# Weighted experts: the first product's 7-for-8 scheme beside the second's, in 64x64 pieces of the array, with packed weights

## The chip, the cores and the metric

The kernel runs on one core of one Trainium2 chip. A time is device microseconds of one execution. TensorE is written PE, its weight loads PEld, VectorE DVE, ScalarE ACT, GpSimd POOL, and SyncE, which issues most DMAs, SP. All data are fp32.

## The reference, cut to what matters

```
q_p, k_p = phi(q), phi(k)                   # 64 features: outer product of two 8-wide projections
x = (q_p @ (k_p.T @ v)) / (q_p @ sum(k_p))  # 4 batches, 4 heads, 1088 tokens, 32 wide
x: (4352, 128)                              # the heads side by side
P = exp(x @ w_gate - max)                   # 8 experts
8 times: P /= row sums; P /= column sums; P *= 4352 / 8
out = sum over e of P[:, e] * (relu(x @ w1[e]) @ w2[e])   # w1 128 x 1024, w2 1024 x 128
```

Every token goes through every expert, so the two products of the experts are nearly all of the arithmetic. Because P is positive, P[:, e] may be multiplied into x ahead of the first product.

## The kernel before

**Layout.** xT holds x transposed: 128 features on the partitions, 4352 tokens along the free axis. The first product of one expert takes 128 columns of w1 as weights and streams tokens: the hidden values come out with 128 of the 1024 hidden units on the partitions. The second product takes 128 rows of w2 as weights and streams hidden values. Every matmul is issued as two halves of 64 output columns, at positions (0, 0) and (0, 64) of the array (128 rows by 64 columns each), and the trace shows each fp32 half as two MATMUL and two LDWEIGHTS instructions.

**Three stretches.** First attention, batch by batch (`attention(b)`), with POOL and SP turning its result into xT (`take_over`, L486 and L488). Then `routing()`: the logits and 8 rounds of row and column sums, small work on DVE. Where attention and routing leave PE free, the generator `steps()` fills in expert work that needs no P (calls of `fill(n)`): expert 0 for all tokens, and expert 1 for the first 1280. This is the plain phase; its results, unweighted, wait in `kept`. At the end of routing P goes to DRAM as `pT`, and the weighted phase does the rest: experts 1 to 7 for the tokens from 1280 on, experts 2 to 7 below. In it x is multiplied by its weights, broadcast from `pT` by a DMA, on POOL (`prepare_x`, L678).

**The weighted phase before.** Groups of 3 tiles of 256 tokens. `four(k)` computes the first product in the ordinary way (`first`, L914), four blocks of 128 hidden units at a time; ACT applies the relu out of PSUM (L918). The second product of 4 hidden blocks by 2 output halves by 3 token tiles would be 24 half-size products; `twenty(k)` does it with 20, from sums of hidden values (DVE, L978 and L998) and sums of blocks of w2 (`sums_of_four`: POOL once for each expert, L242, then stored in DRAM and loaded back for each group). `into` (L1099) accumulates them in PSUM, `part_of_twenty` combines the sums at a group's end. The last group has 2 tiles of 256 and 7 products for 8 in the second product (`seven`), with sums of w2 from `sums_of_two` (POOL, L203 to L206).

**Queues.** DVE, PE and ACT run an order written by hand (`tc.manual_schedule`). POOL and SP are in-order queues. An instruction in `tc.keep_in_program_order(...)` is pinned behind the instruction traced before it on its engine. The buffers of the early phases (`phs`, two tiles, and `rb`) are read by attention until its last matmuls L462, at 96.8 us. The code that runs as routing ends is:

```
        for n in routing():
            fill(n)
        early.close()
        pools.append(ctx.enter_context(tc.tile_pool(name="late", bufs=2)))
        prepare_x(PLAIN)
        fill(8)
    for _ in work:
        pass
```

Of the kernel before, what the change touches and what calls it, by code (L numbers as in the profile page):

```python
# [18 lines left out]
def f64_to_f32(nc, pool, raw, shape):  # L19


    p, n = shape
    low, high = raw[:, 0::2], raw[:, 1::2]

    def u32(name):
        return pool.tile([p, n], U32, name=name)

    def f32(name):
        return pool.tile([p, n], F32, name=name)
# [21 lines left out]
def kernel(  # L51
# [31 lines left out]
    wpool = ctx.enter_context(tc.tile_pool(name="wpool", bufs=2))  # L83
# [5 lines left out]
    hb = big.tile([P, 9600], F32, name="hb")  # L89
    early = ExitStack()  # L90
    ld = early.enter_context(tc.tile_pool(name="ld", bufs=2))
    wk = early.enter_context(tc.tile_pool(name="wk", bufs=2))

# [93 lines left out]
    def load_w(e, sums=True, again=False):  # L187
        w1 = wpool.tile([P, F], F32, tag="w1", name="w1")
        w2 = wpool.tile([P, FO, DM], F32, tag="w2", name="w2")
        nc.sync.dma_start(out=w1, in_=moe_w1[e])  # L190
        nc.sync.dma_start(out=w2, in_=moe_w2[e].rearrange("(fo fi) d -> fi fo d", fi=P))
        return w1, w2, sums_of_two(e, w2, again) if sums else None

    def sums_of_two(e, w2, again=False):

        ws = wpool.tile([P, 4, FO // 2, H2], F32, tag="ws", name="ws")
        if e in stored:
            nc.sync.dma_start(out=ws, in_=stored[e])
            return ws
        a11, a21 = w2[:, 0::2, 0:H2], w2[:, 0::2, H2:DM]  # L200
        a12, a22 = w2[:, 1::2, 0:H2], w2[:, 1::2, H2:DM]
        keep_ = tc.keep_in_program_order if e < 2 else lambda x: x
        keep_(nc.gpsimd.tensor_tensor(ws[:, 0], a21, a22, op=Alu.add))  # L203
        keep_(nc.gpsimd.tensor_tensor(ws[:, 1], ws[:, 0], a11, op=Alu.subtract))
        keep_(nc.gpsimd.tensor_tensor(ws[:, 2], a11, a21, op=Alu.subtract))
        keep_(nc.gpsimd.tensor_tensor(ws[:, 3], a12, ws[:, 1], op=Alu.subtract))  # L206
        if again:
            stored[e] = dram.tile([P, 4, FO // 2, H2], F32, name=f"ws{e}")
            nc.sync.dma_start(out=stored[e], in_=ws)
        return ws  # L210

    stored, stored_four = {}, {}

    FOURS = (((5, 6), ((0, 0), (0, 2)), ((1, 0), (1, 2)), True),
             ((4, 10), ((1, 0), (1, 2)), ((1, 1), (1, 3)), False),
             ((12, 7), ((0, 0), (0, 2)), ((0, 1), (0, 3)), False),
             ((11, 14), ((0, 2), (1, 2)), ((0, 1), (0, 1)), True),
             ((1, 16), ((0, 0), (1, 0)), ((0, 3), (0, 3)), True),  # L220
             ((15, 13), ((0, 1), (0, 3)), ((1, 0), (1, 2)), False),
             ((2,), ((1, 3),), ((0, 3),), True), ((3,), ((1, 1),), ((0, 1),), True),
             ((8,), ((1, 1),), ((1, 2),), True), ((9,), ((1, 3),), ((1, 0),), True))
    FORMS = [n for ns, *_ in FOURS for n in ns]

    def sums_of_four(e, w2):

        ws = pools[0].tile([P, len(FORMS), FO // 4, H2], F32, tag="ws4", name="ws4")
        if e in stored_four:
            nc.sync.dma_start(out=ws, in_=stored_four[e])  # L230
            return ws

        def blocks(bs):
            b = w2[:, bs[0][1]::4, H2 * bs[0][0]:H2 * (bs[0][0] + 1)].unsqueeze(1)
            if len(bs) == 1:
                return b
            step = (bs[1][1] - bs[0][1]) * DM + (bs[1][0] - bs[0][0]) * H2
            return AP(tensor=b.tensor, offset=b.offset, ap=[b.ap[0], [step, 2], *b.ap[2:]])

        c = 0  # L240
        for ns, x, y, off in FOURS:
            tc.keep_in_program_order(nc.gpsimd.tensor_tensor(ws[:, c:c + len(ns)], blocks(x), blocks(y),  # L242
                                                             op=Alu.subtract if off else Alu.add))
            c += len(ns)
        stored_four[e] = dram.tile([P, len(FORMS), FO // 4, H2], F32, name=f"ws4{e}")
        nc.sync.dma_start(out=stored_four[e], in_=ws)
        return ws


# [5 lines left out]
    def projections():  # L255
        flat = raw.rearrange("p n d -> p (n d)")
        s12 = f64_to_f32(nc, consts, flat, (P, 2 * D)) if words == 2 else flat.bitcast(F32)
# [25 lines left out]
    both = consts.tile([P, H2], F32, name="both")  # L283
    nc.gpsimd.tensor_tensor(both, ident[:, 0:H2], ident[:, H2:DM], op=Alu.add)
# [3 lines left out]
    first_w = load_w(0, False)  # L288
# [282 lines left out]
    def routing():  # L571
# [22 lines left out]
        for it in range(ITERS):  # L594
# [7 lines left out]
            nc.vector.reduce_sum(cs, p1.rearrange("p g e -> p e g"), axis=AX.X)  # L602
            yield 4.25
# [13 lines left out]
        for b in (1, 0, 2, 3):  # L617
# [9 lines left out]
    NMAX = 512  # L627
# [4 lines left out]
    groups = [(0, 256, 2, [0], False), (512, 288, 2, [0], False), (0, 256, 2, [1], False),  # L632
              *((1088 + 832 * i, 416, 2, [0], False) for i in range(3)), (3584, 384, 2, [0], False),
              (512, 384, 2, [1], False)]
    PLAIN = len(groups)
# [3 lines left out]
    for lo in (1280, 512, 2048, 2816, 3584):  # L639
        groups.append((lo, NT3, 3, list(range(2 if lo == 512 else 1, E)), True))  # L640
    groups.append((0, 256, 2, list(range(2, E)), True))
    assert sorted((lo, e) for lo, n, t, es, _ in groups for lo in range(lo, lo + n * t, 32) for e in es) == [
        (lo, e) for lo in range(0, N, 32) for e in range(E)]
    kept = [keep.tile([P, N], F32, name="kept0"), keep.tile([P, 1280], F32, name="kept1")]
    items = [(g, e) for g, group in enumerate(groups) for e in group[3]]
    loaded_w, sources, sums, parts, done = {}, {}, {}, {}, {}
# [5 lines left out]
    def tiles_of(j):  # L652
        return groups[items[j][0]][2]

    def prepare_w(j):
        g, e = items[j]
        three = groups[g][2] == 3
        if j == 0:
            loaded_w[j] = first_w
        elif items[j - 1][1] == e or not groups[g][4]:  # L660
            before = [i for i in range(j) if items[i][1] == e and i in loaded_w]
            loaded_w[j] = loaded_w[before[-1]] if before else load_w(e, False)
            if three and tiles_of(j - 1) == 2:
                loaded_w[j] = *loaded_w[j][0:2], sums_of_four(e, loaded_w[j][1])
        else:
            loaded_w[j] = load_w(e, not three, again=groups[g][4])
            if three:
                if g == len(groups) - 2 and e in groups[-1][3]:
                    sums_of_two(e, loaded_w[j][1], True)
                loaded_w[j] = *loaded_w[j][0:2], sums_of_four(e, loaded_w[j][1])  # L670

    def weights_of(e, lo, n, tag):
        pb = pools[0].tile([P, 3 * NT3], F32, tag=tag, name=tag)[:, 0:n]
        tc.keep_in_program_order(nc.sync.dma_start(out=pb, in_=pT[e:e + 1, lo:lo + n].to_broadcast([P, n])))
        return pb

    def weigh(out, x, pb):
        tc.keep_in_program_order(nc.gpsimd.tensor_tensor(out, x, pb, op=Alu.mult))  # L678

    def prepare_x(j):  # L680
        g, e = items[j]
        lo, n, t, es, weighted = groups[g]
        x = xT[:, lo:lo + t * n]
        if not weighted:
            sources[j] = x
            return
        xe = weights_of(e, lo, t * n, "xe")
        for sl in (slice(0, 512), slice(512, 768)) if j == first_weighted else (slice(0, t * n),):
            weigh(xe[:, sl], x[:, sl], xe[:, sl])
        sources[j] = xe  # L690

    first_weighted = next(j for j, (g, e) in enumerate(items) if g == PLAIN)

    def weigh_kept(g, i):

        lo, n, t, es, _ = groups[g]
        ys = [kept[e][:, lo:lo + n * t] for e in range(es[0])]
        if i < len(ys):
            weigh(ys[i], ys[i], weights_of(i, lo, n * t, "pb"))
            return  # L700
        for y in ys[1:]:
            tc.keep_in_program_order(nc.gpsimd.tensor_tensor(ys[0], ys[0], y, op=Alu.add))
        if t == 2:
            k1, k2 = ys[0][upper, 0:n], ys[0][upper, n:2 * n]
            tc.keep_in_program_order(nc.gpsimd.tensor_tensor(k1, k1, k2, op=Alu.subtract))
# [5 lines left out]
    def put(y, lo, n, queues):  # L711
        b0, nb = lo // 32, n // 32
        yt = pools[0].tile([P, NT3 // 32, 32], F32, tag="yt", name="yt", bufs=4)[:, 0:nb, :]
        nc.vector.transpose(out=yt.rearrange("p b d -> p (b d)"), in_=y)
        store(yt, b0, b0 + nb, queues)

    def part(g, k):

        if g in DIRECT:
# [519 lines left out]
    for _ in work:  # L1239
        pass  # L1240
# [30 lines left out]
```

## Time and profile before

| | us |
|---|---|
| median of 3 runs | 920.2 (919.67 to 921.0) |
| span of the profiled execution | 918.0 |
| median less span (what lies around it) | 2.2 |
| PE busy | 911.2 |
| DVE busy | 678.9 |
| ACT busy | 421.6 |
| POOL busy | 204.0 |
| first matmul of the weighted phase starts | 184.2 |

The profile is of one execution; times within it count from the start of its span, and no time of that execution other than its span is given. A row of a group reads: line, engine, operation, written tile <- read tiles, shapes, count | busy us, mean ns of one | idle of the engine just before. A row of the timeline reads: start, duration, engine, line, what, count.

### The profile page before, as it was taken

Reading aid. Unit: us, or ns where it says so; the run is one execution under the profiler, and the core shown is the slowest. Engines: PE = TensorE matmul, PEld = TensorE weight load, DVE = VectorE, ACT = ScalarE, POOL = GpSimd, SP = SyncE. Lnnn points to the kernel's source line nnn. Section 1 sums busy time; section 2 is a strip of 40 time slices with the busy share of each in tenths; the row PEclk is TensorE's granted clock in tenths of the full one; section 3 lists DMA queues with packets and bytes.
Section 4 is the critical chain, followed back from the end, with each engine's and each line's share of the span. In section 5 each row is a group of like instructions: output and inputs, shape, how many; then the busy total and the mean of one; then the engine's idle time right before and its main releaser. Section 6 shows DMA issues by size and latency. Waiting matters only on the chain.

```text
span 918.0 us, 18893 instructions
## 1 busy us (share of the span) xinstructions
PE 911.2 (99%) x7442; PEld 637.4 (69%) x7442; DVE 678.9 (74%) x1173; ACT 421.6 (46%) x915; POOL 204.0 (22%) x212
## 2 busy tenths in 40 slices
PE   9999999999999999999999999999999999999997
PEld 6777544466666677777777777777777655556886
DVE  7678699888776798666975656956567976758665
ACT  3455555554444454444544444544445444445443
POOL 3121100175545421201210010110100243210220
PEclk9999999999999999999999999999999999999999
DMA  9994100213454535534364343454445456453640
GB/s 254 308 273 163 54 1 1 70 64 127 148 150 139 186 119 174 165 110 150 114 185 134 117 143 112 132 187 127 133 122 165 130 170 195 162 166 92 177 153 13
DMA packets 91305, 128.15 MB, mean 140 GB/s; under 512 B 25392, under 2 KB 69504, under 8 KB 86480
## 3 DMA queue, kind: packets, MB, share of 16 engines
q1 hardware_dynamic: 88384, 121.42, 42.7%
q0 software_dynamic: 1600, 5.36, 2.1%
q8 instruction: 58, 0.95, 0.4%
q10 hardware_dynamic: 1232, 0.16, 0.1%
q14 instruction: 31, 0.25, 0.1%
HBM read 107.88 MB, written 19.05 MB: 138 GB/s over the span
## 4 chain that ended last, share of the span: by engine, by line
PE 97%; DVE 2%; ACT 1%; issue 0%; POOL 0%; DVEq 0%; POOLq 0%
PE a L914 51%; PE s L1099 41%; PE a L347 1%; PE a L462 1%; PE a L114 1%; DVE hb L931 1%; PE a L314 0%; PE s L376 0%; PE a L426 0%; PE s L392 0%; DVE cs L602 0%; PE a L496 0%; PE a L392 0%; ACT hb L918 0%; DVE rs L596 0%
## 5 line engine op out<-in xcount | busy, mean ns | idle before, releaser
L914 PE MATMUL a<-xe,w 128*64 128x256 f32 (+1 forms) x2560 | 569.8, 470 | 0.0
L918 ACT ACTIVATE hb<-a 128x256 f32<-128x256 f32 (+4 forms) x408 | 195.0, 480 | 241.5 <-PE a L914 209.3
L914 PEld LDWEIGHTS a<-xe,w 128*64 128x64 f32 x2560 | 263.0, 137 | 50.8 <-issue 1.8
L918 ACT ACTIVATE hx<-a 128x256 f32<-128x256 f32 (+1 forms) x360 | 167.3, 465 | 213.5 <-PE a L914 191.6
L1099 PE MATMUL s<-hb,ws 128*64 128x256 f32 (+3 forms) x1312 | 256.1, 395 | 0.2 <-DVE hb L931 0.2
L1099 PE MATMUL s<-hx,ws 128*64 128x256 f32 x1280 | 233.9, 379 | 0.0
L978 DVE TENSOR_TENSOR hb<-hb 128x512 f32<-128x512 f32 (+1 forms) x204 | 133.5, 664 | 102.8 <-ACT hb L918 98.8
L978 DVE TENSOR_TENSOR hx<-hx 128x512 f32<-128x512 f32 (+1 forms) x204 | 149.8, 744 | 65.0 <-ACT hx L918 60.2
L1099 PEld LDWEIGHTS s<-hb,ws 128*64 128x64 f32 x1312 | 134.9, 137 | 87.8 <-issue 64.5
L678 POOL TENSOR_TENSOR xe<-xT,xe 128x768 f32<-128x768 f32 (+2 forms) x41 | 80.3, 1958 | 481.2 <-DMA xe<-pT 377.0
L1099 PEld LDWEIGHTS s<-hx,ws 128*64 128x64 f32 x1280 | 132.7, 137 | 71.6 <-issue 50.3
L914 PE MATMUL a<-xT,w 128*64 128x416 f32 (+3 forms) x512 | 119.7, 462 | 0.0
L1099 PE MATMUL s<-hb,w 128*64 128x256 f32 (+3 forms) x536 | 114.2, 408 | 0.0
L1099 PE MATMUL s<-hx,w 128*64 128x256 f32 x384 | 76.0, 379 | 0.0
L931 DVE TENSOR_TENSOR hb<-hb 128x416 f32<-128x416 f32 (+7 forms) x84 | 60.7, 723 | 18.0 <-ACT hb L918 14.0
L1099 PEld LDWEIGHTS s<-hb,w 128*64 128x64 f32 x536 | 54.1, 137 | 19.0 <-issue 6.5
L914 PEld LDWEIGHTS a<-xT,w 128*64 128x64 f32 x512 | 48.9, 137 | 25.5 <-issue 15.7
L242 POOL TENSOR_TENSOR ws<-w 128x256 f32<-128x256 f32 (+1 forms) x70 | 60.5, 899 | 8.1 <-DMA w<-in_moe_w_dram 5.2
L931 DVE TENSOR_TENSOR hx<-hx 128x256 f32<-128x256 f32 (+1 forms) x65 | 39.5, 612 | 24.0 <-ACT hx L918 22.8
L1099 PEld LDWEIGHTS s<-hx,w 128*64 128x64 f32 x384 | 40.8, 137 | 6.6
L978 DVE TENSOR_TENSOR pqg<-hb 128x512 f32<-128x512 f32 x68 | 40.5, 637 | 0.0
L978 DVE TENSOR_TENSOR pqg<-hx 128x512 f32<-128x512 f32 x68 | 35.0, 554 | 0.0
(181 smaller groups left out, 485.0 us busy)
## 6 DMA issues: line engine op xcount, KB each, us to landing
w<-in_moe_w_dram SPq DMA_DIRECT2D x82, 512.0 KB, 5.5
ws<-ws SPq DMA_DIRECT2D x34, 1024.0 KB, 5.0
xe<-pT SPq DMA_DIRECT2D x34, 384.0 KB, 4.1
ws<-ws SPq DMA_DIRECT2D x12, 512.0 KB, 3.6
ph<-qa SPq DMA_DIRECT2D x12, 288.0 KB, 4.7
rb<-qb SPq DMA_DIRECT2D x3, 1152.0 KB, 7.2
pb<-pT SPq DMA_DIRECT2D x6, 384.0 KB, 8.3
kx<-in_k_dram SPq DMA_DIRECT2D x4, 544.0 KB, 4.0
```

The lines of the kernel that those rows point to most:

```text
L114: nc.tensor.matmul(warm[:, 0:P], ones, ones, start=True, stop=True)
L242: tc.keep_in_program_order(nc.gpsimd.tensor_tensor(ws[:, c:c + len(ns)], blocks(x), blocks(y), op=Alu.subtract if off else Alu.add))
L347: nc.tensor.matmul(pv[64 * s:64 * (s + 1), i], kp[0:n, H * t + h].rearrange("p i j -> p (i j)"), vx[0:n, slots[h], t, :], start=(t == 0 an ...
L462: nc.tensor.matmul(pn[64 * s:64 * (s + 1), t, 2 * i:2 * i + 2].rearrange("p h d -> p (h d)"), ph[:, i, s, 64 * t:64 * (t + 1)], kvs[b % 2] ...
L678: tc.keep_in_program_order(nc.gpsimd.tensor_tensor(out, x, pb, op=Alu.mult))
L914: nc.tensor.matmul(ph[sl], loaded_w[j][0][:, P * f + H2 * s:P * f + H2 * (s + 1)], sources[j][:, lo:hi], start=True, stop=True, tile_posit ...
L918: nc.scalar.activation(out=out, in_=ph, func=Act.Relu)
L931: nc.vector.tensor_tensor(out, a, b, op=Alu.subtract)
L978: nc.vector.tensor_tensor(out if not isinstance(out, tuple) else places(*out), places(*a), places(*b) if isinstance(b, tuple) else b, op=A ...
L1099: nc.tensor.matmul(sums[g][i][H2 * s:H2 * (s + 1), n * place:n * (place + 1)], w, x, start=c == 1, stop=c == per, tile_position=(0, H2 * s))
```

## The change

Only the weighted phase and what prepares it change; attention, routing and the plain phase compute as before.

- Both products now use 7 half-size products for 8 (Strassen's scheme in Winograd's form). To halve every dimension of the first product too, its contraction of 128 features is split into halves of 64. So all weighted matmuls work on 64x64 pieces of the array, at the row positions 0 and 64 and the column positions 0 and 64. `r` is the row half. Each has PSUM banks of its own: `fbanks[2r]`, `fbanks[2r + 1]` for the first product, two of the four `ysums` for the second.
- The scheme's sums of products in the first product are made in PSUM: PE accumulates, ACT copies a partial sum to a second place (`taps`: tm1, tu2), PE accumulates on; a small matmul of zeros at the start marks the banks as written.
- Groups are 2 tiles of 256 tokens (6 groups, experts 1 to 7), then 208, 224 and 208 (experts 2 to 7). A group with one expert is an item: 42 items of 2 x 256 columns, 18 of 2 x 208 or 2 x 224. An item is 2 units; a unit has, for each r, 7 first and 7 second products of 2 matmuls. `AT` gives the place of every step in a period of 14 slots.
- The weights are rearranged by `pack(e)` for experts 1 to 7, called in the first 7 rounds of routing: 12 DMAs on SP into `phs` and `rb`, 8 sums on POOL, 2 DMAs on POOL's queue that store 896 KB each to `packed[e]`. Each item then loads 2 x 896 KB. `sums_of_four` and the w1, w2 loads of the weighted phase go.
- `turn` swaps the feature halves of the weighted x by DMA, `xsums` makes its sums on POOL.
- The group's end (`group_end`) adds up four sums; the last group no longer folds `kept` into PSUM.

```diff
+    def pool(*args, op):
+        tc.keep_in_program_order(nc.gpsimd.tensor_tensor(*args, op=op))
+    def forms(a11, a12, a21, a22, s1, s2, s3, s4, turn):
+        pool(s1, a21, a22, op=Alu.add)
+        pool(s2, s1, a11, op=Alu.subtract)
+        pool(s3, *((a21, a11) if turn else (a11, a21)), op=Alu.subtract)
+        pool(s4, a12, s2, op=Alu.subtract)
...
+    def pack(e):
+        fs = [phs[i].rearrange("p i n -> p (i n)")[:, 0:28 * H2].rearrange("p (c n) -> p c n", c=7) for i in range(2)]
+        x = rb.rearrange("p i n -> p (i n)")[:, 0:8 * H2].rearrange("p (i n) -> p i n", i=2)
...
+        for form, k, j, jo, io in ((A11, 0, 0, 0, 0), (None, 0, 1, 0, 1), (A12, 1, 0, 1, 0), (A22, 1, 1, 1, 1)):
+            t = at(0, form).rearrange("p (u f) -> p u f", u=2)
+            for r in range(2):
+                k0 = H2 * (k ^ r)
+                tc.keep_in_program_order(nc.sync.dma_start(
+                    out=t[H2 * r:H2 * (r + 1)],
+                    in_=moe_w1[e][k0:k0 + H2, 512 * r:512 * (r + 1)].rearrange("k (u j f) -> k u j f", u=2, j=2)[:, :, j]))
+            tc.keep_in_program_order(nc.sync.dma_start(
+                out=at(1, form).rearrange("p (q d) -> p q d", d=H2),
+                in_=moe_w2[e].rearrange("(q j f) (i d) -> f q j i d", j=2, f=P, i=2)[:, :, jo, io]))
+        for i in range(2):
+            f = fs[i]
+            forms(f[:, A11], f[:, A12], x[:, i], f[:, A22], *(f[:, n] for n in (S1_, S2_, S3_, S4_)), i == 1)
+        packed[e] = dram.tile([2, P, 7, 4 * H2], F32, name=f"packed{e}")
+        for i in range(2):
+            tc.keep_in_program_order(nc.gpsimd.dma_start(out=packed[e][i], in_=fs[i]))
...
             nc.vector.reduce_sum(cs, p1.rearrange("p g e -> p e g"), axis=AX.X)
+            if it < E - 1:
+                pack(it + 1)
             yield 4.25
...
+    AT = {"M1": 1, "M5": 0, "M6": 6, "M2": 5, "M7": 9, "M3": 10, "M4": 13, "tm1": 4.0, "tm5": 4.5, "tu2": 7.5, "c22": 10.5, "c12": 12.0, "rel": 16.5, "r3": 24.5, "stt": 27.5, "ts2": 29.5, "ts3": 32.0, "L": 32}
...
+    def weights(i):
...
+        weights_of(x, e, lo, 2 * n)
+        pool(x, x, xT[:, lo:lo + 2 * n], op=Alu.mult)
+    def turn(i):
+        for r in range(2):
+            tc.keep_in_program_order(nc.sync.dma_start(out=xf(i, Y1, T1)[rows[r]], in_=xf(i, X1, Y1)[rows[1 - r]]))
+    def xsums(i):
+        n = wgroups[witems[i][0]][1]
+        pool(xf(i, T1), xf(i, X2), xf(i, X1), op=Alu.subtract)
+        pool(xf(i, T3, T4), xf(i, Y2, T1).to_broadcast([P, 2, n]), xf(i, X2, T3)[:, 0:4:3], op=Alu.subtract)
+        pool(xf(i, T4), xf(i, Y1), xf(i, T2), op=Alu.subtract)
+    def first_weights(i):
+        w1s[i] = pools[0].tile([P, 7, 2, P], F32, tag="w1f", name="w1f")
+        tc.keep_in_program_order(nc.sync.dma_start(out=w1s[i].rearrange("p i u f -> p i (u f)"), in_=packed[witems[i][1]][0]))
...
+    def first_product(k, r, m):
+        i, u, g, n = unit_of(k)
+        form, x, b, c = FIRST[m]
+        for s in range(2):
+            nc.tensor.matmul(half_of(r, b, c, n)[rows[s]], w1s[i][rows[r], form, u, H2 * s:H2 * (s + 1)],
+                             xf(i, x)[rows[r]], start=m == opens, stop=True, tile_position=(H2 * r, H2 * s),
+                             skip_group_check=True)
+    def taps(k, r, m):
...
+        if m == "tm1":
+            nc.scalar.copy(b, a)
+        elif m == "tm5":
...
+            nc.scalar.copy(m5s[k, r], c)
+        elif m == "tu2":
+            nc.scalar.copy(d, a)
+        elif m == "rel":
+            nc.scalar.activation(out=h[:, H0:H2_ + 1:H2_, r], in_=fbanks[2 * r + 1][:, 0:2 * n].rearrange("p (c n) -> p c n", c=2),
+                                 func=Act.Relu)
+        elif m == "c12":
+            nc.vector.tensor_tensor(h[:, C12, r], a, m5s[k, r], op=Alu.add)
+        elif m == "c22":
+            nc.vector.tensor_tensor(h[:, H3, r], d, m5s[k, r], op=Alu.add)
...
             fill(n)
         for n in routing():
             fill(n)
-        early.close()
-        pools.append(ctx.enter_context(tc.tile_pool(name="late", bufs=2)))
-        prepare_x(PLAIN)
-        fill(8)
-    for _ in work:
-        pass
+        weights(0)
+        turn(0)
+        xsums(0)
+        for _ in work:
+            pass
+    early.close()
+    pools.append(ctx.enter_context(tc.tile_pool(name="late", bufs=2)))
+    first_weights(0)
+    second_weights(0)
...
+        for _, _, call in weighted_events():
+            call[0](*call[1:])
```

In `hsums` ACT applies one more relu (r3, 2n columns) and DVE makes the second product's sums: stt (4n columns), ts2 and ts3 (2n each). `weighted_events` sorts all steps by `14 * unit + 9 * r + AT`; second products fill the slots from 32 on that the unit's r leaves free.

## The prediction

> **What bounds the kernel now.** I read the page first: busy time by engine and the chain that ended last.
>
> ```profile
> PE 911.2 (99%) x7442; PEld 637.4 (69%) x7442; DVE 678.9 (74%) x1173; ACT 421.6 (46%) x915; POOL 204.0 (22%) x212
> ...
> PE 97%; DVE 2%; ACT 1%; issue 0%; POOL 0%; DVEq 0%; POOLq 0%
> ```
>
> PE is busy 99% and the chain is 97% PE: fewer slots on PE shorten the kernel, and any idle PE lengthens it one for one. A busy PE need not be at its peak, so next the price of a slot, from the pieces of the chain inside the weighted phase (start, length, line, instructions):
>
> ```profile
> 406.18 0.86 PE s L1099 x8
> ...
> 425.13 0.86 PE s L1099 x8
> ```
>
> The same place of two successive items (768 tokens of one expert) lies 18.95 us apart. An item has 8 x 3 slots of first product and 2 x 20 half products, 20 slots, so 44 slots of 256 columns: 0.4307 us each. In the timeline at the end of the plain phase, pairs of 384 columns follow at 182.26, 182.91 and 183.56: 0.65 each, so a slot goes with its columns (1.683 ns each), with nothing to add. Two rows of the groups by shape speak of small pieces of the array:
>
> ```profile
> L376 PE MATMUL s<-qT,wq 64*128 64x512 f32 x8 | 2.0, 615 | 0.0
> L347 PE MATMUL a<-v,kp 128*64 128x64 f32 x256 | 8.7, 223 | 0.0
> ```
>
> L376 uses the two row halves of the array, on different banks: 8 matmuls of 512 columns in 2.0 us, where one after another at 0.43 they would take 3.4. L347 is short: its timeline has 28 matmuls with their loads in 0.99 us, about 30 ns for a pair of instructions.
>
> Then I looked at who is idle while routing runs, since the change puts the packing there (the timelines of POOL and SP around it, and the stretch by windows):
>
> ```profile
> 98.91 2.20 POOL L488 DMA_DIRECT2D xT<-xd  x4 [3.43 <-DMA xd<-xt]
> 179.98 3.02 POOL L678 TENSOR_TENSOR xe<-xT,xe 128x512 f32<-128x512 f32 x2 [78.87 <-PE s L1099]
> ...
> 101.19 1.75 SPq L488 DMA_DIRECT2D xT<-xd  x4
> ...
> 103.00:184.00 81.00, 80.78 (x519) 36.50 (x517) 69.73 (x125) 47.79 (x98) 4.02 (x4) 1.00 0.09 22
> ```
>
> POOL and SP come free at 101.1 and 102.9; PE has plain work until 184.2, 81 us later. That window, with POOL (fifth figure) and DMA (0.09) idle, is what the packing has.
>
> **The change part by part. PE's work.** Removed: 34 items x 18.95 = 644.3, and the last group, 6 experts x (16 + 14) slots x 0.4307 = 77.5; together 721.8. Added: a unit has 7 + 7 tasks for each row half, so 14 slots if both row halves run side by side; an item 28. 42 items x 28 x 0.4307 = 506.5; for 208 columns a slot is 0.350, for 224 0.377, so 6 x (2 x 9.80 + 10.56) = 181.0. Sum 687.5: 34.3 saved. No row shows four 64x64 pieces at once. Bounds: 687.5, or twice that if the row halves took turns; L376 is the nearest row, so I take 687.5. Instructions: 8 matmuls and 8 loads a slot, 54 ns a pair, against 30 in L347.
>
> [...]
>
> **ACT and DVE in a unit of 6.03 us.** ACT: 6 copies of 256 at 0.372 (row L750, 373), 2 relus and r3 of 512 at 0.60: 4.0. DVE: 4 adds of 256 at 0.42, one of 1024 at 1.22 (L331), two of 512 at 0.75 (L978): 4.4. Both below PE. The new waits are what may cost: M6, ACT's tu2, then M7 three slots later, and whatever is queued behind M7 on PE waits too. From M6's start to M7's: a slot 0.431, the end of its pipeline 0.163 (a 256 matmul lasts 379 ns, the next starts after 216), 0.095 to ACT (490.607 to 490.705 in the trace), the copy 0.372, again 0.095, a load not hidden 0.104: 1.26 against 3 x 0.431 = 1.29. It fits by 0.03. With 208 columns 1.13 against 1.05: 0.08 late, twice a unit, 36 units: 6 us. An ACT copy into PSUM has no row; between 0 (copies as before) and 25 us (0.1 late twice a unit) I take 6, from the rows of 372.
>
> **The packing.** Everything is pinned: POOL does pack 1 to pack 7, and only then the first weighted x (`weights(0)`), which M1 needs. SP's loads of pack e + 1 go into `phs`, which the two stores of pack e must have read: one chain, no double buffer. One round:
> - stores: issue 0.7, 1,792 KB. The row of a 1,024 KB load is 4.7 us to landing in a quiet window, 3.5 of it data, so 300 GB/s: 896 KB land 4.2 after issue, the second 3.1 later: 8.0. Bounds 6.0 (446 GB/s, the best slice) and 10.
> - loads: the third DMA needs the second store, the 11th the sums: 8 issues x 0.43 (1.75 for 4, above) and 2.1 to landing (48 KB row): 5.5. Bounds 4.4 and 7.4.
> - 8 sums of 128x256: rows
>
> ```profile
> L203 POOL TENSOR_TENSOR ws<-w 128x256 f32<-128x256 f32 x8 | 5.9, 735 | 48.8 <-DMA w<-in_moe_w_dram 48.8
> L242 POOL TENSOR_TENSOR ws<-w 128x256 f32<-128x256 f32 x42 | 42.1, 1035 | 8.1 <-DMA w<-in_moe_w_dram 5.2 <-PE a L914 2.9
> ```
>
> I take 0.90, between them: 7.2. Bounds 5.8 and 9.4 (1.18, the longest).
>
> A round is 20.7 us (16.2 to 26.8). Pack 1 starts when SP is free: 103.0 + 10 x 0.43 + 2.1 + 7.2 = 116.6. Pack 7's sums end at 116.6 + 6 x 20.7 = 240.8. Then on POOL two store issues 1.3 and the product with 512 weights 1.4 (row 1,384 ns): 243.5; on SP, pinned behind that, `turn`'s two issues 0.9, then the load of the first weights, 4.3: PE starts the weighted phase at 248.7. It has no other work from about 189 (184.2 and the last second products of the plain phase, 7 slots x 0.65) until then. Packs 2 to 7 are not needed for another 12 us each, but the queue holds expert 1 behind them.
>
> [...]
>
> **The ends.** At the end the last unit's second row half runs 9 slots later (3.2), then the relu, stt, ts2, ts3 and 7 slots of second products, of which about 5.0 stand alone: 8.2. `group_end`: copies 0.5, two adds 1.2, nine short DVE adds 3.6 (rows of 0.42 at 256), two ACT copies 0.6, transpose 0.6, store 2.1: 8.6, where 5.0 was. In the steady state a group's end hides under the next group's matmuls. Item DMAs, 2.3 MB in 12.1 us, are 195 GB/s against 140 before; they hide, as each is issued 12 slots (5 us) or more ahead and lands in about 5. `sums_of_four` on POOL cost nothing before (PE never waited for it), so its going brings nothing.
>
> **Sum.** 248.7 start + 687.5 + 6 + 8.2 + 8.6 = 959.0 span; with 2.2 around it 961.2. The median before is its span plus that 2.2. By this sum the break-even start would be 207.7, a round of 13.9 us, below the low corner of 16.2. All low ends together give 923, all high ends 1,025.
>
> **Rivals.**
> - *Faster: the packing does not hold the start back.* Some of the chain runs ahead of my reading (another order on POOL or SP, buffers free earlier), so the first weights are there when plain work ends. PE then starts at 189 and the time is 189 + 687.5 + 6 + 8.2 + 8.6 + 2.2 = 901.5. It decides from a round under 13.9 us. For it: 81 us of idle POOL and DMA. Against: sums alone take 5.8 or more a round, and two landings follow them.
> - *Slower still: PE waits for its own partial sums.* If ACT's PSUM to PSUM copy costs as much as the row of 512 (598 ns, 0.226 more), M7 comes 0.2 late twice a unit: 0.4 x 120 = 48 us, so 1,003. It decides from a copy over 0.40 us. Against: copies of 256 out of PSUM are steady at 364 to 385.
> - *The pieces do not run side by side.* 687.5 more: about 1,650. L376 speaks against it.
>
> **How the numbers follow.** My forecast has 0.78, the late start being worked out from four rows with all corners on one side. The faster rival has 0.12, since the order of pinned queues is read from the code and not from a trace; PE's waits 0.08; the turns 0.02. A measurement of this kernel can tell about 0.2% from no change. Faster by more: 0.11; within: 0.01 (the faster rival with half its start given back); slower: 0.88. The range leaves out the faster rival, the turns and the far corners: 926 to 1,006.
>
> **What would show it.** PE nearly idle from 189 to about 249 in the slices, while POOL works in 7 bursts of 7 us some 21 us apart, with two stores and twelve loads between; then items of 12.06 us. PE slots of 0.43 with four pieces would confirm the saving; a gap ahead of M7 the waits. If PE has no gap near 190, or the bursts come under 14 us apart, the forecast is wrong.

## The result, and the profile after

The changed kernel takes 1013.1 us (median of 4 runs, 1012.28 to 1015.39) against 919.93 (919.65 to 921.0): 1.1014 times the time before, 95% interval 1.0998 to 1.103. The prediction was 961.2, its range ended at 1,006. It had the direction and the largest cause; 52 us are missing.

From the page of the changed kernel: busy time, two rows of slices, the instruction queue's row, and the chain by engine.

```profile
PE 921.7 (91%) x15264; PEld 761.1 (75%) x15264; DVE 756.7 (75%) x1229; ACT 536.3 (53%) x1350; POOL 389.8 (39%) x391
...
PE   9999989800799999999999999999999999999996
...
PEclk9999999955699999999999999999999999999998
...
q8 instruction: 120, 1.97, 0.8%
...
PE 76%; DVE 7%; DMA 7%; POOL 4%; SPq 3%; issue 2%; ACT 1%; POOLq 0%; DVEq 0%; ACTq 0%
```

PE's share of the chain fell from 97% to 76%. The two zeros in PE's slices are the late start that was foreseen. The windows view gives that stretch in one line (start and end, length, then busy time and count of PE, PEld, DVE, ACT, POOL, then the granted clock as a share of full speed, the busy share of the DMA engines and GB/s):

```profile
198.00:258.00 60.00, 0.86 (x8) 0.00 (x0) 3.96 (x6) 2.08 (x5) 24.66 (x34) 0.54 0.52 171
```

The timelines of POOL, SP and PE show its end: the last pack's sums, its stores, the first weighted x, its turn, and the first weights, which SP issues only 2.4 us after it is done with the turn. It waits there for the second store of pack 7, which lands 6.03 us after its issue, at 252.54: the tiles for the weights come from the pool `late`, opened behind `early.close()`, and `phs` belongs to the pool that this closes. The two pieces of the chain come last.

```profile
240.28 0.72 POOL L199 TENSOR_TENSOR ph<-rb,ph 128x256 f32<-128x256 f32 x1 [12.76 <-DMA ph<-in_moe_w_dram]
...
245.94 1.10 POOL L242 DMA_DIRECT2D packed<-ph  x2
247.06 1.27 POOL L199 TENSOR_TENSOR xf<-xf,xT 128x512 f32<-128x512 f32 x1
```

```profile
248.36 1.94 SPq L888 DMA_DIRECT2D xf<-xf  x2
252.73 0.35 SPq L898 DMA_DIRECT2D w1f<-packed  x1
```

```profile
258.23 1.97 PE L931 MATMUL a<-xf,w1f 64*64 64x256 f32 x8 [59.37 <-DMA w1f<-packed]
```

```profile
246.51 6.03 DMA packed<-ph
...
252.73 4.60 DMA w1f<-packed
```

Then the slot. Two pieces of the chain at the same place of successive units (start, length, line, instructions):

```profile
396.99 0.86 PE s L980 x16
...
403.03 0.86 PE s L980 x16
```

They stand 6.04 us apart: 14 slots of 0.4314. The four 64x64 pieces work side by side at the old price of a slot. Counting first products in the trace, 56 to a unit, gives every unit's length. The first 84 units (256 columns) take 531.3 us where the sum had 506.5; the 35 intervals of 208 and 224 columns take 201.5, where the slots alone are 176. Most units take 6.04, but the first takes 10.40, around each group's end they read 6.48, 6.44, 8.21, 6.25, 6.16, and those of 208 columns scatter from 4.97 to 7.2 against 4.90.

The first unit stands in the row PEclk above: the granted clock is 0.50 from 203.3, some 4 us after PE has run out of work, until 271.5. The windows view of the first 13.3 us of the weighted phase and of what follows:

```profile
258.20:271.50 13.30, 12.00 (x80) 6.10 (x84) 1.70 (x4) 4.25 (x12) 5.97 (x6) 0.50 0.60 211
271.50:300.00 28.50, 28.24 (x492) 24.76 (x488) 23.10 (x32) 17.00 (x43) 12.37 (x9) 1.00 0.55 185
```

A product of 256 columns takes 631 ns in the median in the first stretch and 376 later.

What PE stood still for between 262 and 985 us is in the waits ahead of weight loads (what was waited for: us in all, times, longest):

```profile
PEld a L931 <- issue: 6.4, 15, 1.4
PEld s L980 <- issue: 6.1, 7, 1.8
PEld a L931 <- ACT a L945: 5.9, 17, 1.3
PEld s L980 <- DVE ht L965: 4.3, 5, 1.4
PEld s L980 <- DVE hb L965: 4.0, 6, 1.3
PEld a L931 <- DVE ht L952: 3.3, 7, 0.7
PEld a L931 <- ACT m L943: 2.3, 7, 0.5
PEld a L931 <- DVE ht L950: 2.0, 4, 1.1
PEld a L931 <- DVE hb L950: 2.0, 5, 0.6
```

With the shorter rows that follow, DVE has 17.5 us, "issue" (nothing that the profile names) 12.5, ACT 9.9. Here L945 is tu2, L943 tm5, L952 and L950 are c22 and c12, L960, L963 and L965 are stt, ts2 and ts3, and L1010 is the adds of `group_end`.

### The profile page after: what moved, and what is told of

It is laid out like the page before. It is cut to its first block, busy times and chain, and to the rows that moved or that the text cites. A ratio compares the mean times of both kernels' runs of the same rounds, so it can differ in the third digit from the quotient of the medians.

```text
span 1012.1 us, 36092 instructions
## 1 busy us (share of the span) xinstructions
PE 921.7 (91%) x15264; PEld 761.1 (75%) x15264; DVE 756.7 (75%) x1229; ACT 536.3 (53%) x1350; POOL 389.8 (39%) x391
## 4 chain that ended last, share of the span: by engine, by line
PE 76%; DVE 7%; DMA 7%; POOL 4%; SPq 3%; issue 2%; ACT 1%; POOLq 0%; DVEq 0%; ACTq 0%
PE a L931 33%; PE s L980 32%; PE a L736 4%; DMA packed<-ph 4%; POOL ph L199 4%; PE s L798 3%; SPq L231 2%; DVE zs L1010 2%; DMA ph<-in_moe_w_dram 1%; PE a L338 1%; SPq L234 1%; DVE ys L1010 1%; DVE ht L960 1%; PE a L453 1%; DVE hb L960 1%
## 5 line engine op out<-in xcount | busy, mean ns | idle before, releaser
L931 PE MATMUL a<-xf,w1f 64*64 64x256 f32 (+2 forms) x6720 | 533.0, 371 | 64.9 <-DMA w1f<-packed 59.4
L931 PEld LDWEIGHTS a<-xf,w1f 64*64 64x64 f32 x6720 | 352.0, 133 | 119.0 <-issue 67.4
L980 PE MATMUL s<-ht,w2f 64*64 64x256 f32 (+2 forms) x3360 | 274.5, 366 | 4.2 <-DVE ht L965 2.1
L980 PE MATMUL s<-hb,w2f 64*64 64x256 f32 (+2 forms) x3360 | 271.4, 366 | 4.2 <-DVE hb L965 2.1
L199 POOL TENSOR_TENSOR xf<-xf 128x256 f32<-128x256 f32 (+2 forms) x180 | 210.3, 1168 | 142.7 <-DMA xf<-xf 96.5
L980 PEld LDWEIGHTS s<-ht,w2f 64*64 64x64 f32 x3360 | 194.7, 133 | 18.5 <-DVE ht L965 4.3
L980 PEld LDWEIGHTS s<-hb,w2f 64*64 64x64 f32 x3360 | 191.3, 133 | 20.8 <-DVE hb L965 4.7
L945 ACT COPY a<-a 128x256 f32<-128x256 f32 (+2 forms) x240 | 83.1, 346 | 177.3 <-PE a L931 177.3
L952 DVE TENSOR_TENSOR ht<-a,m 128x256 f32<-128x256 f32 (+2 forms) x120 | 48.9, 407 | 131.2 <-PE a L931 68.1
L940 ACT COPY a<-a 128x256 f32<-128x256 f32 (+2 forms) x240 | 84.0, 350 | 98.2 <-PE a L931 72.6
L952 DVE TENSOR_TENSOR hb<-a,m 128x256 f32<-128x256 f32 (+2 forms) x120 | 48.9, 408 | 67.8 <-PE a L931 67.5
L943 ACT COPY m<-a 128x256 f32<-128x256 f32 (+2 forms) x240 | 89.8, 374 | 0.4 <-issue 0.3
L960 DVE SCALAR_TENSOR_TENSOR hb<-hb 128x1024 f32<-128x1024 f32 (+2 forms) x60 | 84.6, 1409 | 1.4 <-ACT hb L947 1.2
L960 DVE SCALAR_TENSOR_TENSOR ht<-ht 128x1024 f32<-128x1024 f32 (+2 forms) x60 | 83.1, 1386 | 0.2
```

The lines of the kernel that those rows point to most:

```text
L199: tc.keep_in_program_order(nc.gpsimd.tensor_tensor(*args, op=op))
L931: nc.tensor.matmul(half_of(r, b, c, n)[rows[s]], w1s[i][rows[r], form, u, H2 * s:H2 * (s + 1)], xf(i, x)[rows[r]], start=m == opens, stop= ...
L940: nc.scalar.copy(b, a)
L943: nc.scalar.copy(m5s[k, r], c)
L945: nc.scalar.copy(d, a)
L952: nc.vector.tensor_tensor(h[:, H3, r], d, m5s[k, r], op=Alu.add)
```

## The experiments

Times are medians. The changed kernel is at 1013.1 and the kernel before at 919.7 to 920.8 in every comparison. "Start" is the first weighted product.

### Why the weighted phase starts late

**One pack for all experts.**

```diff
-            if it < E - 1:
-                pack(it + 1)
+            if it == 0:
+                pack(1)
+                packed.update({e: packed[1] for e in range(2, E)})
```

> Leaves out packs 2 to 7: experts 2 to 7 use expert 1's packed weights. The packing is then one round (12 loads, 8 sums, 2 stores) in place of seven. Theory H1 (the one-buffered chain of packs holds expert 1 back): the first weighted product starts when the plain phase's last work ends, about 190 to 200 instead of 258, and the time falls by 55 to 65 us, to 950 to 958. Rival (the start is late for another cause, such as the P matrix, the turn or the loading of the first weights): the start stays above 240 and the time within 10 us of 1,013. In both, the units after the start are as in the changed kernel (6.04 us at 256 columns), so the weighted phase's own 44 us over the sum stay.

954.93 us, 58 less; start at 198.1. The units are as before (531.9 and 203.6 us), the first one's 10.40 us too: the granted clock is 0.50 here from 198.1 to 211.7. The chain of packs is the late start, and the loss inside the phase is another thing.

**Two sets of packing buffers**, one for odd and one for even experts.

```diff
+        if e % 2:
+            fs, x = [ph[0][:, 0:28 * H2], ph[1][:, 0:28 * H2]], r[:, 0:8 * H2]
+        else:
+            fs, x = [r[:, 8 * H2:36 * H2], spare[0][:, 0:28 * H2]], ph[0][:, 28 * H2:36 * H2]
```

> Computes all; the packs alternate between two sets of buffers (the second in the rest of the rb tile, a third tile and the rest of the ph tile), so that a pack's loads and sums need not wait for the stores of the one before. H1 (the one set of buffers sets the round of 21 us): the bursts of POOL's sums come 9 to 13 us apart, pack 7 ends between 170 and 200, the first weighted product starts at 198 to 212, and the time is 955 to 970. Rival (POOL's and SP's queues or DRAM set the round, not the buffers): rounds of 18 us or more, a start after 230 and a time above 985.

968.45 us, start at 211.6. POOL's bursts begin at 113.0, 121.9, 138.9, 147.6, 163.8, 172.2 and 188.1: pairs, some 25 us to a pair, where one round took 21. The single set of buffers was the price. The start is not yet at 198, and it is no longer the packs that hold it: SP is done with the turn at 199.9, pack 7's second store lands at 202.58, and the weights, issued at 206.03, wait longest for the last second products of the plain phase on PE (205.96), as SP's waits show:

```profile
SPq L905 <- PE s L805: 2.8, 1, 2.8
```

The plain phase itself ends at 197.8 in the changed kernel, at 192.9 with one pack and at 206.0 here. Why its end moves so was not tried.

### What holds PE up inside the phase: leaving parts out

**The weighted x made only for three items.**

```diff
+            if i > 2:
+                at(b + FORMS_AT, lambda i: xforms.update({i: xfs[i % 3]}), i)
```

> Leaves out the weighted x of all items but the first three: their three tiles are used again, so POOL's product and sums, the broadcast of P and the turn are gone from the weighted phase, while PE, ACT and DVE do all that they did. Theory H2 (POOL's operations stretch DVE's sums in SBUF, and PE waits for DVE at group ends and in the small groups): the sum of 1,024 columns stays at 1.22 us and those of 512 at 0.69 throughout, units of 208 columns come to 4.9 to 5.2 us, and the time falls by 20 to 35 us, to 978 to 993. Rival R1 (PE waits for ACT's copy between M6 and M7): units of 208 and 224 columns stay at 5.7 us in the mean and the time within 6 us of 1,013.

988.79 us: 24 less. In this run stt takes 1.22 and ts2 and ts3 0.69 nearly throughout. But the run takes the DMAs of x away too, and of the waits ahead of weight loads "issue" falls most, to 1.1 us from 12.5, DVE's part only to 13.6 from 17.5; the two are told apart further down. The changed kernel's timelines show what POOL does to DVE. DVE in two successive units, and POOL:

```profile
403.32 1.22 DVE L960 SCALAR_TENSOR_TENSOR ht<-ht 128x1024 f32<-128x1024 f32 x1
404.57 0.69 DVE L963 TENSOR_TENSOR ht<-ht 128x512 f32<-128x512 f32 x1
...
408.66 0.42 DVE L952 TENSOR_TENSOR hb<-a,m 128x256 f32<-128x256 f32 x1 [1.27 <-PE a L931]
409.02 0.42 DVE L950 TENSOR_TENSOR hb<-a,m 128x256 f32<-128x256 f32 x1
409.36 1.57 DVE L960 SCALAR_TENSOR_TENSOR hb<-hb 128x1024 f32<-128x1024 f32 x1
410.96 1.10 DVE L963 TENSOR_TENSOR hb<-hb 128x512 f32<-128x512 f32 x1
```

```profile
402.47 0.73 POOL L199 TENSOR_TENSOR xf<-xf 128x256 f32<-128x256 f32 x1
408.57 1.28 POOL L199 TENSOR_TENSOR xf<-xf,xT 128x512 f32<-128x512 f32 x1 [5.37 <-PE a L931]
409.92 1.59 POOL L199 TENSOR_TENSOR xf<-xf 128x256 f32<-128x256 f32 x1
```

POOL alone takes 0.73 for 256 columns and DVE 1.22 and 0.69; together, 1.59, 1.57 and 1.10. The adds at 408.66 and 409.02 beside POOL's product keep their 0.42; one operand of theirs (`a`) is in PSUM, while stt, ts2 and ts3 have theirs in SBUF. Over the 256-column phase the median of stt is 1,216 ns with no POOL instruction beside it and 1,602 with one all along; of ts2 and ts3 692, 1,103 with a partial overlap and 1,648 with a full one; of c12 and c22 424, 424 and 425. The adds of a group's end (L1010) divide in the same way: 256 columns with both operands in SBUF take 0.42 with no POOL instruction beside them and 1.29 and 1.49 with one, 512 columns with one operand in PSUM 0.67 and 0.68. That the place of the operands is the cause was not tried by itself.

**The group's end without its sums.**

```diff
-                for step in range(17):
+                for step in (0, 1, 2, 3, 15, 16):
```

> Leaves out steps 4 to 14 of the end of each group (3 copies on ACT, 8 sums on DVE); what is stored is not the group's sum. H2, its part on the group ends (13 more operations in DVE's in-order queue make DVE late for the units around): the units around a group's end exceed the steady one by about 1 us in all instead of 3.2, and the time falls by 10 to 20 us, most at the three small groups and by about 2 in the tail. Rival R1: only the tail's 3 to 4 us go.

995.96 us, 17 less, 3 of it in the tail (18.1 us from 21.1). The 84 units take 520.4 for 531.3, the small ones, where most was expected, only 3.5 less. DVE's share of the waits is 6.8 us for 17.5.

**Without tu2.**

> Leaves out the copy tu2 on ACT between M6 and M7 (the hidden sums lack a term), so that M7 need not wait for ACT. R1 (M7 is late because its place is three slots behind M6): the units of 208 and 224 columns fall by 0.2 us each or more and the time by 6 to 25 us, to 988 to 1,007. H2: PE waits for DVE, not for that copy: the time falls by 0 to 3 us.

The edit takes "tu2" out of the list of taps. 1006.87 us, 6.2 less, and the waits ahead of weight loads for ACT fall from 9.9 to 1.6. That is about the 6 us that the prediction gave to this wait, but not where it put them. The units of 208 and 224 columns take 198.1 for 201.5, 0.1 a unit and not 0.2; the first 84 take 525.8 for 531.3, and 3.1 of that lie in the first five units. In the changed kernel, too, 3.5 of the 5.9 us ahead of weight loads for tu2 fall between 263 and 275 us, and only 2.0, in 12 waits of 0.15 to 0.18, in the units of 208 and 224.

### Moving things instead

**M6 ahead of M2, and tu2 with it; then M6 alone.**

```diff
-    "M6": 6, "M2": 5, ... "tu2": 7.5
+    "M6": 5, "M2": 6, ... "tu2": 6.5
```

> Computes all; M6 and M2 change places (slots 5 and 6), tu2 comes a slot earlier in ACT's order, so that M7 stands four slots behind M6. Theory A (three slots are too short, as leaving out tu2 suggested): units of 208 columns that nothing else disturbs go from 4.96 or 5.12 us to 4.91, and the time falls by 4 to 7 us, to 1,006 to 1,009. Theory B (leaving out tu2 helped because ACT had less to do): the time falls by 0 to 2 us.

1074.12 us, with most 256-column units at 6.55 and 6.63. ACT's timeline in this run shows what the new place of tu2 did:

```profile
401.39 0.36 ACT L945 COPY a<-a 128x256 f32<-128x256 f32 x1 [1.34 <-PE a L931]
401.66 0.60 ACT L947 ACTIVATE hb<-a 128x512 f32<-128x512 f32 x1
402.29 0.36 ACT L940 COPY a<-a 128x256 f32<-128x256 f32 x1
```

tu2 of one row half now stands ahead of the relu of the other (the tie at 16.5 had put the relu first). It waits 1.34 us for PE with the relu, tm1 and tm5 behind it in ACT's queue, and PE waits for tm5: 37.0 us ahead of weight loads, where the changed kernel has 2.3. "Issue" grew as much, to 37.3 us from 12.5; what that is here was not found.

> Computes all; M6 and M2 change places on PE, and ACT's order stays as it was (the run before that moved tu2 too, ahead of another unit's relu on ACT). Theory A (three slots between M6 and M7 are too short): undisturbed units of 208 columns at 4.91 to 4.96, the time lower by 3 to 7 us. Theory B (no effect of that wait): within 2 us of the changed kernel. Theory C (what made the run before slow was M6's place on PE, not ACT's order): again units of 6.6 us and some 1,070 in all.

With ACT's order as it was, 6.04 is back, but the time is 1023.21, 10 more than the changed kernel. PE's waits for tm5 (L943) grew from 2.3 to 12.1 us, those for tu2 (L945) fell from 5.9 to 4.7. The slot that M7 gained was lost ahead of M6. None of the theories had this. A reading that fits both runs, and was not tried by itself: M6 adds to `a`, in the bank from which tm5 reads `c`; M2 writes the other bank, and its slot used to cover tm5.

**The end's steps 10 slots apart; then the second products 6 slots later.**

```diff
-   (step - 3) * (0.1 if last else 3)
+   (step - 3) * (0.1 if last else 10)
```

> Computes all; steps 4 to 16 at a group's end stand 10 slots apart instead of 3 (not in the last group). H2 with DVE's in-order queue as the cause: the unit of 8 us after each group's end comes to 6.0 to 6.5, and the time falls by 8 to 15 us, to 998 to 1,005. Rival (the same operations cost the same wherever they stand, because DVE has no room in any unit): less than 4 us, the loss only spread over more units.

1002.11 us, 11 less; the unit after a group's end falls from about 8 to 6.04 to 6.3.

```diff
-   "L": 32
+   "L": 38
```

> Computes all; the second products of a unit stand 6 slots later on PE (38 for 32), with DVE's and ACT's order for the hidden sums as it was, so that PE asks for the sums 2.6 us later. If PE waits for DVE's sums ahead of the second products: the unit of 8 us after a group's end comes to 6.1 to 6.6, units of 208 to about 5.2 in the mean, and the time falls by 15 to 30 us less 2.6 in the tail. Rival (PE waits ahead of the first products, for banks that DVE's late adds c12 and c22 still read): less than 5 us.

1012.49 us: nothing, as the rival said. DVE and then PE's weight loads at a group's end in this run:

```profile
372.65 0.69 DVE L965 TENSOR_TENSOR ht<-ht 128x512 f32<-128x512 f32 x1
373.36 1.40 DVE L1010 TENSOR_TENSOR zs<-zs,xs 64x256 f32<-64x256 f32 x1
374.78 0.42 DVE L952 TENSOR_TENSOR ht<-a,m 128x256 f32<-128x256 f32 x1
```

```profile
375.26 0.84 PEld L931 LDWEIGHTS a<-xf,w1f 64*64 64x64 f32 x18 [1.70 <-DVE ht L952]
```

An add of the end, 1.40 us for 0.42 beside a POOL instruction, stands ahead of c22 (L952). PE's first product into the half of the bank that c22 reads waits for it, here for 1.70 us. Room ahead of the second products does not help a wait ahead of the first ones.

**So the order in DVE's queue**: ts3 behind the other row half's c22 and c12, and then the end's sums into such places too.

```diff
-   "ts3": 32.0, "L": 32
+   "ts3": 35.5, "L": 38
```

> Computes all; as the run with late second products (38 for 32), and ts3 at 35.5 for 32 in DVE's order: behind the second row half's c22 and c12 instead of just ahead of them. Theory (PE's first products wait for c22, which waits in DVE's queue behind stretched sums): the late second products, worth nothing alone, now bring 10 to 25 us, 988 to 1,003. Rival (DVE has too little room whatever the order): less than 5 us.

1007.96 us: 5 less, below the 10 to 25 expected and at the rival's edge, though the waits for DVE fall from 17.5 to 9.6.

```diff
-   tops[1] + 4.5 + (step - 3) * 3
+   tops[1] // 7 * 7 + 8 + 7 * (step - 3)
```

> Computes all; the run before, and steps 4 to 16 of a group's end 7 slots apart at the places 8 and 1 of the period of 14, behind c12 and ahead of ts2 (3 apart anywhere before). Same theory: the units around a group's end come to 6.1 to 6.5, another 8 to 15 us below the run before: 978 to 995. Rival: no better than the spread of 10 slots alone, 1,002.

1003.94 us, no better than the spread alone. But the waits ahead of weight loads tell where the gain went (these are the largest rows, and the two left for DVE):

```profile
PEld a L931 <- issue: 13.2, 21, 2.1
PEld s L980 <- issue: 8.8, 10, 1.7
PEld a L931 <- ACT a L945: 7.5, 24, 1.3
...
PEld a L931 <- DVE ht L952: 1.7, 4, 0.6
PEld a L931 <- DVE hb L952: 0.3, 1, 0.3
```

DVE's part is 2.0 for 17.5: the order was what turned stretched sums into idle PE. "Issue" went from 12.5 to 22.0 and took most of it back.

### What "issue" is

One of the longest such waits in the changed kernel, on PE (length, then the idle time ahead in brackets):

```profile
858.03 0.36 PE L931 MATMUL a<-xf,w1f 64*64 64x224 f32 x2
859.44 0.74 PE L980 MATMUL s<-hb,w2f 64*64 64x208 f32 x10 [1.05 <-issue]
```

No semaphore stands there. Counted along PE's instructions, matmuls, loads and the rest, 7 gaps of over 0.35 us from one start to the next in the changed kernel, 8.3 us together, come at one and the same place of every 256 instructions, and 13 of them (13.7 us) in the last run above. Each ends 1.2 to 1.6 us after a packet of the instruction queue (16 KB) has landed. All 7 lie between 846 and 967 us, in the units of 208 and 224 columns, where the same number of instructions is worked off in less time. In the kernel before the row of that queue (packets, MB, busy share of the DMA engines) reads:

```profile
q8 instruction: 58, 0.95, 0.4%
```

The two traces hold 14,994 and 30,903 records of PE and PEld: 259 to a packet before, 258 now. That PE waits in these gaps for its own instructions is a reading of the places and times; no row of the profile says it. Whether other transfers have a part in it was tried by leaving some out.

**The x without its DMAs, POOL kept** (on old data).

> Leaves out the DMAs of the weighted x (the broadcast of P and the turn) of all items but the first three, and keeps POOL's product and sums, on old data. It splits what the run with reused x took away. H2 (POOL's instructions stretch DVE's): the time stays within 8 us of the changed kernel, at 1,005 or more, and DVE's sum of 1,024 columns still shows 1.6 us where POOL runs. Rival (the DMAs or the waits for them were the cost): most of the 24 us go, to about 990.

1038.35 us: slower by 25, which neither theory had. Issue falls to 2.3 us, but DVE's part rises to 50.8. Without DMAs to wait for, POOL's four instructions of an item follow each other closely and fall on the sums of one unit:

```profile
404.01 2.16 DVE L961 SCALAR_TENSOR_TENSOR ht<-ht 128x1024 f32<-128x1024 f32 x1
406.20 1.10 DVE L964 TENSOR_TENSOR ht<-ht 128x512 f32<-128x512 f32 x1
407.34 1.81 DVE L966 TENSOR_TENSOR ht<-ht 128x512 f32<-128x512 f32 x1
```

5.07 us for 2.60, and every second unit takes 7.21. The cost of POOL is not its busy time but where it falls.

**The weights loaded only for three items.**

```diff
+        if i > 2:
+            w1s[i] = w1s[1 + i % 2]
+            return
```

> Leaves out the loads of the packed weights of all items but the first three (their tiles are used again): 1.8 of 2.3 MB of each item's DMAs. PE, ACT, DVE and POOL do all that they did. Theory (some 12 us of PE's idle time are instructions that the instruction queue's DMAs bring late, behind the other transfers): the idle time ahead of weight loads put down to issue falls from 12.5 us to below 4, that for DVE stays at 14 to 22, and the time falls by 6 to 14 us, to 999 to 1,007. Rival (the fetch is late whatever the other DMAs do, or issue is something else): issue stays at 9 or more and the time within 4 us.

1000.35 us, 12.7 less, with POOL's instructions still there. The two rows of "issue" in this run:

```profile
PEld a L937 <- issue: 1.7, 6, 0.7
...
PEld s L986 <- issue: 1.3, 1, 1.3
```

3.0 us for 12.5, DVE's part at 15.5, as the theory said. So these waits hang on the transfers, but not on the weights' alone: with all loads of weights in place, "issue" is 2.3 us without the x's DMAs and 1.1 without the whole making of x.

**The x's DMAs without POOL's work.**

> Leaves out POOL's product and sums for the weighted x of all items but the first three; the DMAs that broadcast P and turn the halves stay, on data without meaning. Theory (POOL costs through DVE's stretched sums, the DMAs through late instructions): issue stays at 9 to 16 us, DVE's part falls from 17.5 to 13.6 or less, as in the run with reused x, and the time falls by 4 to 14 us, to 999 to 1,009. Rival (both parts of the loss hang on POOL): as the run with reused x, issue near 1 and a time of 985 to 993.

993.79 us, 19 less, more than the theory's 4 to 14. DVE's part falls to 12.1 as it should, but issue falls too, to 5.5 where 9 to 16 was expected. The bytes are the same (193 GB/s in the mean for 189), but the gaps at the one place of 256 are 5 for 7 and 4.4 us for 8.3. So the two are not independent: with no POOL work to wait for, the x's transfers can be issued at other times. How much of "issue" hangs on the times of the transfers and how much on their bytes stays open.

### Together

> Computes all; the three edits of this series together (two sets of packing buffers, M6 ahead of M2, the end's steps 10 slots apart). If the three costs are separate, the gains add: 48 + 5 + 11 = 64 us with some 10 either way, a time of 940 to 960, still over the kernel before because of DVE's stretched sums. If they overlap (the same idle time of PE counted twice), 960 or more.

1019.86 us, because M6's move is in it: 54 below that move alone (1074.12), where the other two had brought 45 and 11. The gains add.

> Computes all; two sets of packing buffers, M6 ahead of M2 on PE alone, the end's steps 10 slots apart, and the second products 6 slots later. If the gains add: 45 from the packing, 5 from M6, and 15 to 30 from the other two together, so 935 to 950; the kernel before at 920 is not reached, since the start of the weighted phase at 212 alone is 4 over the break-even.

973.73 us, over the range expected, for M6's move cost 10 instead of bringing 5 and the late second products brought nothing. The single runs add up to 967; the other 7 are not explained.

> Computes all; the run before with two sets of packing buffers. If the causes add: 45 us below the run before, 933 to 950. If not: less than 35 below it.

958.66 us, above the range that was named, but 45 below the same order with one set of buffers: separate causes again. It is 1.042 times the kernel before (1.0386 to 1.0453), and 54 below the change as it was.

> Computes all; the run before with more plain work called in each round of routing (5.25 slots for 4.25), because PE was idle for some 10 of the 60 us from 120 to 180 with two sets of buffers. Theory (the plain work's end sets the start at 212): the start comes 4 to 8 us earlier. Rival (the weights' chain behind pack 7 on POOL and SP sets it): the start moves by less than 2 us or comes later, as routing itself is delayed by more work ahead of it in the queues.

961.11 us, start at 215.1 for 212.9: the rival. The theory was right about the run before, where the first weights waited for the plain phase (207.2, issued at 207.29). With more plain work in each round the plain phase ends at 203.9, but pack 7 comes later: its second store lands at 207.83 for 203.83, and the weights, issued at 208.57, now wait for that. No version here beats the kernel before.

## Why the prediction was right and wrong

- **The slot: right.** 0.4314 for 0.4307, a unit at 6.04, so the saving on PE is real. The loads, 133 ns a piece in the mean and 8 to a slot, fit under the matmuls.
- **The packing chain: right in mechanism, short by 9.5.** Pack 7's sums ended at 245.9 for 240.8: pack 1's 3.3 late, then 21.0 a round for 20.7. In the round of pack 7 the loads behind the last store took 7.7 for 5.5 (SP's issues cost 0.6 each and not 0.43) and the two stores 6.2 for 8.0, so errors cancelled. From there to the first product took 12.3 for 7.9: SP issued the weights 2.4 after it was done with the turn, not at once, since the sum gave nothing to the landing of pack 7's stores ahead of them, and they took 5.5 to the first product. One pack gave the 58 us back.
- **M6, tu2 and M7: the wait is there, its size and place were wrong.** 6 us were foretold for the units of 208 and 224 columns. There the row for L945 has 2.0 us, and leaving tu2 out brought 3.4. That the whole row has 5.9 and the run without tu2 gained 6.2 is luck: more than half of the row falls in the first units after the start. The rival built on a slow copy is out: tu2 and tm1 took 0.357 and 0.361 in the mean. That its number, 1,003, lies near the result is chance.
- **DVE "below PE": the step that failed.** The 4.4 us a unit came from L331, beside which POOL never ran, and from the mean of L978, which hides two prices. The trace of the kernel before had both, in DVE and POOL:

```profile
398.51 2.08 DVE L978 TENSOR_TENSOR hx<-hx 128x256 f32<-128x256 f32 x1 [0.87 <-ACT hx L918]
...
407.99 0.42 DVE L978 TENSOR_TENSOR hb<-hb 128x256 f32<-128x256 f32 x1 [0.87 <-ACT hb L918]
```

```profile
398.49 1.82 POOL L678 TENSOR_TENSOR xe<-xT,xe 128x768 f32<-128x768 f32 x1 [16.16 <-DMA xe<-pT]
```

Beside POOL stt takes up to 2.3 and ts2 and ts3 1.1 to 1.8, and the sum of busy time says nothing of order: c22 frees a bank for PE and stands behind ts3 and the end's adds. PE waited 17.5 us for DVE ahead of weight loads; with the order changed it was 2.0.

- **"A group's end hides under the next group's matmuls": wrong.** It hides on PE and delays DVE. Its nine adds were counted in the tail (21.1 us from the last unit's start, as the sum had it) and not at the eight other ends, where leaving the sums out brought 14 us.
- **What was not in the sum at all: PE's instructions.** 8 matmuls and 8 loads a slot were priced at 54 ns a pair and found short enough; no wait ahead of them was priced. "Issue" is 12.5 us in the changed kernel, 9.5 of it gone when the weights' loads are; the gaps at the one place of 256 are 8.3.
- **Nor was the clock after the idle stretch.** The first unit's 4.4 us over 6.04 stand in rows at a granted clock of 0.50, and are not DVE's, which is busy for 1.70 of those 13.3 us. With one pack the phase starts in the same way (10.40 us, 0.50 from 198.1 to 211.7), so neither run tells the clock's part from that of a first unit that has no second products to put into its waits.
- **The total.** Start +9.5, units of 256 columns +24.8, smaller ones +19.4 beyond the 6, tail -0.6, around the span -1.2: 51.9, and 961.2 + 51.9 = 1013.1. Of the 24.8, 4.4 are the first unit's. The faster rival's 901.5 was out of reach: the plain phase ended at 192.9 at the earliest and not at 189, and with the start at 198 the time was 954.9.

## What to carry to other kernels

A sum of busy times under the period is not enough for an in-order engine: ask which of its instructions frees a buffer for the bottleneck, what stands ahead of it, and how long that takes when POOL runs beside it; here another order took PE's waits for DVE from 17.5 us to 2.0. When a change cuts matmuls into smaller ones, count instructions as traffic too: the instruction queue went from 58 packets to 120 here, and "issue" fell from 12.5 us to 3.0 when the loads of the change's own weights were left out. Work that is "done early in idle time" on one set of buffers has a round time of its own, 21.0 us here, and the first consumer stands behind all rounds if the queue says so. A buffer that a later stage takes over is such a queue too: its first load waits for the last reader, here 2.4 us.

## What the hardware showed that was not expected

- Two DVE operands in SBUF beside a POOL instruction: 692 ns become 1,103 to 1,648 and 1,216 become 1,602 in the median; with one operand in PSUM, 424 stays at 424 to 425. POOL pays too: 0.73 becomes 1.59.
- PE passes one place in every 256 of its instructions 106 times in the weighted phase, and at 7 of them the step from one start to the next is 0.5 to 1.7 us: 8.3 us, with 189 GB/s in the mean. With the weights loaded for three items alone it is one gap of 1.3 us with 87 GB/s. Density alone does not decide it: 4.4 us in 5 gaps with 193 GB/s (no POOL work for x) and none with 165 (x reused).
- After PE's idle stretch before 258 us the granted clock stays at 0.50 for 13.3 us of new work: 631 ns for a product of 256 columns, 376 later.
